# Batch 0 of an attention and token-mixing kernel: w_tok loaded ahead of heads 4 to 7, token mixing on scaled input, both channel-1 halves ahead of channel 2, scores in pairs

## The chip, the cores and the metric

The kernel runs on one core of one Trainium2 chip. The metric is device time in microseconds (us); a kernel's time is the median of its runs. The engines are called as in the profile: PE (TensorE, matrix multiplications), DVE (VectorE), ACT (ScalarE), POOL (GpSimd) and SP (SyncE, which here only issues transfers). Each works through a line of instructions of its own; in the traces below an instruction that waits holds up those behind it on its line (DVE once for 6.83 us). PSUM tiles are the buffers that matmuls write to. The profile is one execution recorded by the hardware profiler.

A run is called fast, or slow when it lies over 1.5% above the fastest run of the same kernel. A ratio below is the mean time of one kernel's fast runs over that of the kernel before's fast runs of the same session, so it is not quite the ratio of the medians that stand beside it. An interval in brackets is a 95% interval.

## The reference, cut to what matters

Four batches, 8 heads, 768 positions, head size 64, model width 512, hidden width 2048.

```python
# block-sorted attention
for _ in range(5):                        # on the 8x8 matrices P (Sinkhorn)
    P = exp(P - max(P)); P /= P.sum(-1) ; P /= P.sum(-2)
k_sorted = einsum('bhij,bhjcd->bhicd', P, k_blocks)       # the same for v
x = softmax(q_block @ k_sorted_block.T / 8) @ v_sorted_block
# mixing, on x of shape (4, 768, 512)
a1  = alpha1 * x + beta1
tok = einsum('ts,bsd->btd', w_tok, a1)                    # token mixing
u   = x + lam * tok
ch  = relu((alpha2 * u + beta2) @ w_ch1) @ w_ch2          # channel 1 (h), channel 2 (ch)
out = u + lam * ch
```

## The kernel before

The program is written out in PE's order. Batch 0 runs as fast as its inputs arrive; from then on the channel mixing of one batch is interleaved with the attention of the next. Cuts are marked.

The loads of batch 0, all issued by POOL, one behind the other: q, then v and k (each in two halves of four heads), then w_tok.

```python
load_q(0)
load_raw(0, 1)              # v, heads 0-3, heads 4-7
load_raw(0, 0)              # k, heads 0-3, heads 4-7
# ...
pool.dma_start(wt16[0:96, :, :], moe_w_tok[0:TAIL, :]. ...)
pool.dma_start(wt16[96:128, :, :], moe_w_tok[TAIL:S, :]. ...)
```

The head of the program. `sc0(h4, g, n)` and `pv0(h4, g, n)` are scores and value sums of a pair of heads; `n` is a number of filler matmuls (identity times identity, thrown away) ahead of them.

```python
mix_k0(0); mix_k0(1)
sc0(0, 0, 1); turn_v0(1, dve.tensor_copy); sc0(0, 1, 1)
mix_k0(2)
pv0(0, 0); sc0(1, 0, 1); turn_v0(2, dve.tensor_copy); pv0(0, 1); sc0(1, 1, 1)
mix_k0(3)
# ... sort_wtok (DVE copies wtp<-wt) and prep_wtok (transposes of w_tok) ...
prep_affine()               # two POOL operations, a1l and b1l
# ...
pv0(3, 0, 2)
# ...
pv0(3, 1, 2)
prep_rs()                   # row sums of w_tok, 36 matmuls with a column of ones
```

Token mixing multiplies plain x; scaling and the row term come afterwards. POOL prepares `u = b1l * rs + x` ahead of time, DVE does the rest.

```python
def moe_tok(b, kts, done=False):
    # ... tok_part(b, kt): 6 matmuls 128x512 into tok_ps, then
    dve.tensor_tensor(tps, tps, a1lB[:], ALU.mult)
    dve.tensor_tensor(u32[kt][:], tok_of[(b, kt)], u32[kt][:], ALU.add)
    act.copy(u16_of[b][:, kt, :], u32[kt][:])
```

The softmax here doesn't subtract the row's maximum and nothing guards it: scores larger than these inputs give would overflow.

## Time and profile before

| | before |
|---|---|
| time, median (range) | 269.02 us (268.73 to 269.40) |
| span of the profiled run | 266.8 us |
| PE busy | 257.3 us, 96% |
| first real work of PE (projection pj) | 11.34 us |
| first token-mixing matmul (tok0) | 33.80 us |
| first channel-1 matmul (h) | 42.47 us |
| last matmul ends | 262.49 us |

The page of the profile first gives each engine's busy time, then the span in 40 slices of 6.7 us: a digit is the busy share in tenths, and PEclk is the clock granted to PE in tenths of full speed. From the page of the kernel before:

```profile
PE 257.3 (96%) x2049; PEld 141.6 (53%) x2059; DVE 154.8 (58%) x333; ACT 125.8 (47%) x232; POOL 92.6 (35%) x100
PE   7799999999999999999999999999999999999993
PEclk9999999999999999999999999999999999999999
```

PE is full in all slices but the first two and the last, and its clock is never lowered. The chain of waits that ended last agrees:

```profile
PE 89%; ACT 4%; DVE 4%; issue 1%; DMA 1%; DVEq 0%; ACTq 0%
```

The next view gives busy time in stretches of the run: from the projection to the first token mixing (tok0), to h, to the token mixing of batch 2 (tok2; tok1 is that of batch 1), to that of batch 3 (tok3), and to the last matmul. Columns: length; busy us of PE, of weight loads, of DVE, ACT and POOL; granted clock; DMA share; GB/s. The kernel before:

```profile
11.34:33.80 22.46, 20.91 (x404) 16.06 (x405) 16.96 (x39) 14.54 (x23) 10.97 (x15) 1.00 1.22 220
33.80:42.47 8.67, 8.67 (x55) 4.20 (x52) 7.14 (x15) 5.79 (x10) 7.78 (x8) 1.00 1.16 210
42.47:143.86 101.39, 100.87 (x809) 55.86 (x813) 64.52 (x129) 53.37 (x100) 44.03 (x45) 1.00 1.07 152
143.86:202.64 58.78, 58.47 (x420) 30.71 (x420) 35.11 (x71) 28.25 (x53) 16.43 (x13) 1.00 0.42 71
202.64:262.49 59.85, 59.69 (x322) 31.04 (x323) 21.98 (x38) 19.95 (x40) 4.16 (x4) 1.00 0.19 49
```

From h on PE is busy for 219.0 of 220.0 us. In the head, the loads set the pace: about 210 GB/s throughout. Two lines of the kernel before's timeline (start, duration), the DVE copies that sort w_tok and the token mixing of batch 1:

```profile
24.53 0.97 DVE L65 COPY wtp<-wt 128x1152 f16<-128x1152 f16 x2
...
85.09 7.93 PE L65 MATMUL tok_ps<-x,w_tokT 128*128 128x512 f16 x36
```

### The profile page before, as it was taken

How to read it: one execution, taken by the hardware profiler on the slowest of the kernel's cores; microseconds unless marked ns; L12 is line 12 of the kernel's file. 1: busy time of each engine (PE TensorE's matmuls, PEld its weight loads, DVE VectorE, ACT ScalarE, POOL GpSimd, SP SyncE). 2: the span in 40 equal slices, each digit the busy share in tenths (PEclk: the TensorE clock that was granted, in tenths of full speed). 3: DMA queues.
4: the chain of work that ended last, by engine and by line, in shares of the span. 5: the costliest groups of instructions: out<-in, count | busy, mean ns of one | idle time of the engine just before them, and what ended most of it. 6: DMA issues, size and time to landing. Idle time of an engine off the chain costs nothing.

```text
span 266.8 us, 5147 instructions
## 1 busy us (share of the span) xinstructions
PE 257.3 (96%) x2049; PEld 141.6 (53%) x2059; DVE 154.8 (58%) x333; ACT 125.8 (47%) x232; POOL 92.6 (35%) x100
## 2 busy tenths in 40 slices
PE   7799999999999999999999999999999999999993
PEld 3467745565565444554565444554565445545542
DVE  6878687639567966722585867704675962042033
ACT  3376767642585312980375404970474305505600
POOL 8524789103585615008918125002409000000000
PEclk9999999999999999999999999999999999999999
DMA  6999999989999544499996342492200422012012
GB/s 80 183 208 252 206 211 207 209 209 118 206 165 146 115 83 120 115 83 95 207 196 135 61 100 80 118 109 51 81 1 2 86 71 79 2 39 79 2 39 79
DMA packets 62423, 30.88 MB, mean 116 GB/s; under 512 B 48888, under 2 KB 58112, under 8 KB 62400
## 3 DMA queue, kind: packets, MB, share of 16 engines
q0 software_dynamic: 23024, 15.60, 39.1%
q1 hardware_dynamic: 39376, 14.96, 32.7%
q8 instruction: 16, 0.26, 0.4%
q14 instruction: 7, 0.06, 0.1%
HBM read 32.78 MB, written 8.65 MB: 155 GB/s over the span
## 4 chain that ended last, share of the span: by engine, by line
PE 89%; ACT 4%; DVE 4%; issue 1%; DMA 1%; DVEq 0%; ACTq 0%
PE ch_ps L65 31%; PE h_ps L65 30%; PE tok_ps L65 12%; PE x_ps L65 5%; PE sc_ps L65 4%; ACT kT L65 2%; PE v_ps L65 2%; PE k_ps L65 1%; PE q_ps L65 1%; ACT et L65 1%; DVE csum L65 1%; DVE P L65 1%; PE m_ps L65 1%; DVE rsum L65 1%; PE wtok_ps L65 1%
## 5 line engine op out<-in xcount | busy, mean ns | idle before, releaser
L65 PE MATMUL h_ps<-a2T,W1p 128*128 128x384 bf16 x512 | 93.4, 326 | 0.2
L65 ACT ACTIVATE hTa<-h_ps 128x384 bf16<-128x384 f32 x96 | 45.9, 492 | 67.7 <-PE h_ps L65 66.6
L65 PE MATMUL ch_ps<-W2p,hTa 128*128 128x512 bf16 (+2 forms) x290 | 65.9, 370 | 0.5
L65 PEld LDWEIGHTS <-W1p 128*128 128x128 bf16 x512 | 47.5, 98 | 30.3 <-issue 0.9
L65 DVE TENSOR_TENSOR ch_ps<-ch_ps,lamB 128x512 f32<-128x512 f32 (+2 forms) x25 | 16.9, 676 | 62.8 <-PE ch_ps L65 60.1
L65 POOL TENSOR_SCALAR u<-b1lB,rs 128x512 f32<-128x512 f32 x18 | 28.9, 1612 | 64.7 <-DVE ost L65 60.1
L65 PEld LDWEIGHTS <-hTa 128*128 128x128 bf16 x300 | 28.7, 98 | 32.4
L65 PE MATMUL tok_ps<-x,w_tokT 128*128 128x512 f16 x144 | 32.1, 379 | 0.0
L65 POOL TENSOR_TENSOR u<-x,u 128x512 f32<-128x512 f16 x22 | 25.4, 1190 | 18.2 <-DVE x L65 17.3
L65 ACT ACTIVATE et<-sc_ps 96x768 f16<-96x768 f32 x32 | 24.9, 807 | 11.7 <-PE sc_ps L65 11.7
L65 ACT CAST u<-u 128x512 f16<-128x512 f32 x24 | 14.8, 618 | 25.7 <-DVE u L65 25.7
L65 PE MATMUL ch_ps<-W2p,hTb 128*128 128x512 bf16 (+2 forms) x100 | 25.0, 371 | 0.0
L65 PEld LDWEIGHTS <-w_tokT 128*128 128x128 f16 x180 | 14.8, 97 | 16.1
L65 DVE TENSOR_TENSOR tok_ps<-tok_ps,a1lB 128x512 f32<-128x512 f32 x24 | 16.6, 693 | 7.7 <-PE tok_ps L65 7.6
L65 DVE CAST kT<-k_ps 64x512 f16<-64x512 f32 x24 | 16.5, 688 | 3.4 <-PE k_ps L65 3.0
L65 DVE TENSOR_TENSOR x<-x_ps,recip 96x512 f16<-96x512 f32 (+2 forms) x32 | 17.6, 554 | 0.9
L65 DVE TENSOR_TENSOR u<-tok_ps,u 128x512 f32<-128x512 f32 x24 | 16.4, 689 | 1.7
L65 ACT ACTIVATE hTb<-h_ps 128x384 bf16<-128x384 f32 x32 | 15.3, 497 | 3.8 <-PE h_ps L65 3.4
L65 DVE TENSOR_TENSOR ost<-ch_ps,u 128x512 f32<-128x512 f32 (+2 forms) x25 | 16.6, 665 | 0.6
L65 POOL DMA_DIRECT2D qn<-in_q_dram x18 | 15.4, 872 | 4.2 <-PE q_ps L65 3.4
L65 PEld LDWEIGHTS <-hTb 128*128 128x128 bf16 x100 | 9.6, 98 | 10.9
L65 PEld LDWEIGHTS <-et 96*128 96x128 f16 (+2 forms) x288 | 12.4, 99 | 4.6 <-issue 1.2
(95 smaller groups left out, 214.0 us busy)
## 6 DMA issues: line engine op xcount, KB each, us to landing
out_dram<-ost SPq DMA_DIRECT2D x23, 192.0 KB, 2.2
raw<-in_v_dram POOLq DMA_DIRECT2D x8, 384.0 KB, 8.2
raw<-in_k_dram POOLq DMA_DIRECT2D x8, 384.0 KB, 10.7
vscr<-vA SPq DMA_DIRECT2D x6, 384.0 KB, 4.4
Vs<-vscr SPq DMA_DIRECT2D x6, 384.0 KB, 7.5
W1p<-in_moe_w_ch_dram POOLq DMA_DIRECT2D x4, 512.0 KB, 10.5
W2p<-in_moe_w_ch_dram POOLq DMA_DIRECT2D x4, 512.0 KB, 18.6
qn<-in_q_dram POOLq DMA_DIRECT2D x12, 128.0 KB, 5.8
```

What stands on the lines that cost most here:

```text
L65: ins = getattr(self.eng, name)(*args, **kwargs)
```

## The change

Its intent is to have real work in place of fillers in the head, and less work on DVE and POOL: w_tok is wanted earlier, so its transposes can fill PE's gaps; token mixing can start on the first columns while the last pair of heads is unfinished; and `a1 = alpha1*x + beta1` is applied to the input (`xa`, times lam and scaled up by 1024, meant to keep the precision of the small factors in f16), which makes row sums, the row term and two POOL operations per tile needless. Scores go in pairs of 16 matmuls, so that PE enters a group of scores half as often. The diff, cut to its core:

```diff
+    LAM_UP = 1024.0
-    load_q(0)
-    load_raw(0, 1)
-    load_raw(0, 0)
+    load_q0(0)                       # then the identity is built, then q's other parts
# ... seven fillers ahead of the projection gone; two groups of q's transposes moved ahead of it
+    load_raw0(0)                     # k and v, heads 0-3
     pool.dma_start(wt16[0:96, :, :], ...)
     pool.dma_start(wt16[96:128, :, :], ...)
+    load_raw0(1)                     # k and v, heads 4-7
# ... fillers of the head gone; scores of batch 0 in pairs; POOL scales heads 0-3:
+        if h4 < 3:
+            aff0(h4 - 1, pool)
+    def affine(b, lo, hi, eng, kts=slice(0, NT)):
+        eng.tensor_tensor(xa, x, a1l16[:, lo:hi] ..., ALU.mult)
+        eng.tensor_tensor(xa, xa, b1l16[:, lo:hi] ..., ALU.add)
# ... batches 1 to 3: scaling on DVE behind the last heads of attention
         def gather(lo, hi):
             for a in range(3):
                 dve.tensor_copy(x128[96:128, a:a + 4:3, lo:hi], ...)
+            affine(b, lo, hi, dve)
# ... token mixing
-                dve.tensor_tensor(tps, tps, a1lB[:], ALU.mult)
-                dve.tensor_tensor(u32[kt][:], tok_of[(b, kt)], u32[kt][:], ALU.add)
+            dve.scalar_tensor_tensor(
+                u32[kt][:], tok_of[(b, kt)], 1.0 / LAM_UP, x_of[b][:, kt, :], op0=ALU.mult, op1=ALU.add
+            )
# ... batch 0: column halves, PSUM tiles shared by kt 0/1 and 2/3
+    for kt in range(NT):
+        tok_part(0, kt, 0, C // 2)
# ... order behind h(0,0)
-    for kk in range(2):
-        moe_ch(0, 0, (kk,))
-        mix_k(1, gs=((0, 1), (2,))[kk])
-        for h4 in range(2 * kk, 2 * kk + 2):
-            turn_q(1, h4, dve.tensor_copy)
+    for n in range(3):
+        moe_h(0, 1, range(2 * n, 2 * n + 2))
+        mix_k(1, gs=(n,), share=(2, 0, 2))
+        turn_q(1, n, dve.tensor_copy)
+    turn_q(1, 3, dve.tensor_copy)
```

## The prediction

> **What bounds it now.** TensorE. The page has PE busy 257.3 of 266.8 us, and the chain of waits is 89% PE. By the timeline, PE starts real work at 11.3 us (the normalised sort matrix is ready), token mixing at 33.8 us, channel-1 (h) at 42.5 us; its last matmul starts after 262.1 us and the last store is issued at 264.2 us. From 42.5 to 262.5 us (220.0 us) PE is nearly gapless: counts times start-to-start times (128x384 0.1625 us, 128x512 0.216, scores 0.039, ...) give about 214 us, so only some 6 us are overhead there. The largest named part is entering a group of scores: 24 entries cost 3.7 us, 0.10 us each where nothing else waits, 0.3 us where a PSUM buffer is late. [...] Before 42.5 us PE is padded with filler matmuls, and the DMA engines are full from about 4 us on, at some 0.2 MB/us.
>
> **Removed from PE before h.** Ten filler matmuls (about 2.3 us), 36 row-sum matmuls (0.9 us), two q transposes' groups moved into the normalisation, small idle gaps: about 3.7 us, if nothing else waits.
>
> **Added before h.** (a) The identity is built after one DMA issue (0.78 us), and DVE copies `pick` before the first reduction: normalisation ends about 0.5 us later. (b) w_tok (1.18 MB) now goes ahead of heads 4 to 7. Landings before: q 9.7, v 13.7, k 17.6, w_tok 23.5 us. At the same rate heads 4 to 7 land at about 21.4 us (k) and 23.2 us (v), where k and v were complete at 17.6. PE, in order, should idle 2 to 3 us at the mixing of k for pair 2. Behind v there are still about 17 us of PE work to h. (c) With both column halves of token mixing ahead of the transposes, the first h waits about 0.5 us for a2T. Summed with trace durations, h starts at about 42.9 us (41.5 to 44.2), against 42.5: the saving is eaten by the DMA order.
>
> **After h starts.** Paired scores: 12 entries for 24; 3.7 us become about 2.2 us ([...]some waits of the second pair for two exponentials of 0.7 us each): -1.3 us. DVE loses one 0.69 us operation per token tile and gains f16 scaling; POOL loses nearly all (54 us): off the critical path, worth about 0. Both channel-1 halves first: same PE work; W2 needed later. Tail: the last two stores go out on two queues: -0.4 us.
>
> **Sum.** +0.4 -1.3 -0.4 = about -1.3: 267.6 us, range 264.9 to 270.6. Faster by over 2%: 0.08; within: 0.88; slower: 0.04.
>
> **What would show it.** Right: a PE wait of 2 us or more for DMA before m_ps near 19 to 21 us; first h between 41.5 and 44; sc groups of 16 entered 12 times after h starts, at about 0.10 us, with fewer us lost than before; DVE and POOL busy much lower without effect; last store on ACT's queue. Wrong: no DMA wait at m_ps, h starting by 40 us.
>
> **What would make it wrong.** The DMA stream starting or running faster than before (then up to 3 us more gain, near 264); long waits of token mixing for POOL's scaling (two 128x768 operations per pair, estimated 2 us each from 1.2 us for 128x512), or of W1's last parts, whose issue stands behind that POOL work; paired scores waiting longer for PSUM.

Two passages are cut out of it: a sentence that gave a reason for the 0.10 us of an entry into scores, which no run here shows, and, in the bracket behind "about 2.2 us", the term of 12 entries at that 0.10 us, 1.2 us in all. The sum is +0.4 us to h, -1.3 us for paired scores and -0.4 us for the tail, about -1.3 us, so 267.6 us (3.7 less 2.2 us is 1.5; 1.3 went into the sum). The 0.10 us itself is in the trace of the kernel before: counted from the start of the matmul ahead and the usual spacing of its kind, scores start 0.09 us late in the median of the 24 entries behind h, 0.29 us at most. The exponentials of scores there take 0.81 us each, 0.70 us from start to start.

## More of the kernel before

Output goes through two buffers, and its stores go out on SP's queue, the one that also carries the transposes of q and of u.

```python
ost = att.tile([128, C], FT, name="ost", tag="ost", bufs=2)
# ... 16 matmuls into cps (ch_ps)
dve.tensor_tensor(cps[:], cps[:], lamB[:, lo:hi], ALU.mult)
dve.tensor_tensor(ost[:, lo:hi], cps[:], u_of[b][kt][:, lo:hi], ALU.add)
nc.sync.dma_start(out[b, kt * 96:(kt + 1) * 96, lo:hi], ost[0:96, lo:hi])
nc.sync.dma_start(out[b, TAIL + kt * 32:TAIL + (kt + 1) * 32, lo:hi], ost[96:128, lo:hi])
```

## The result, and the profile after

The changed kernel takes 293.22 us (292.17 to 296.61, 4 runs) against 269.20 us beside it; the ratio is 1.088 [1.084, 1.092]. The prediction, 267.6 us with a range to 270.6, was 25.6 us too low. The change also spread the times: the four runs of the kernel before beside it lie within 0.7 us; the changed kernel, run twice, ranges from 287 to 297 us.

Both profiles of the changed kernel fell on runs that are called slow by the rule above (296.6 us, and 293.8 us in the second session).

The page of the changed kernel:

```profile
PE 263.5 (89%) x2038; PEld 150.7 (51%) x2051; DVE 149.4 (51%) x324; ACT 127.2 (43%) x232; POOL 42.5 (14%) x62
PE   6787897899899958969999999989999899999994
PEclk9968559999999977999999999999999999999999
```

The work saved is there: POOL fell from 92.6 to 42.5 us, DVE from 154.8 to 149.4. But PE has holes all along the first half, and in slices 3 to 6 and 15, 16 its clock is lowered. The chain that ended last has lost its simplicity:

```profile
PE 51%; DMA 18%; DVE 16%; ACT 6%; POOL 5%; issue 2%; SPq 1%; DVEq 0%; ACTq 0%; POOLq 0%
```

The same stretches as above, in the changed kernel:

```profile
12.60:41.49 28.89, 23.66 (x347) 19.68 (x347) 20.50 (x40) 15.53 (x23) 14.18 (x16) 0.63 1.03 169
41.49:54.38 12.89, 10.47 (x87) 8.55 (x86) 5.15 (x14) 3.09 (x5) 2.28 (x4) 0.89 1.18 204
54.38:169.82 115.44, 103.56 (x808) 56.73 (x814) 61.83 (x129) 55.87 (x105) 15.09 (x22) 0.97 1.05 114
169.82:230.74 60.92, 57.55 (x415) 30.64 (x419) 34.00 (x69) 28.48 (x52) 0.00 (x0) 1.00 0.52 83
230.74:290.60 59.86, 59.70 (x321) 31.04 (x324) 18.27 (x32) 19.42 (x38) 0.00 (x0) 1.00 0.19 49
```

Three stretches lost: to tok0 6.4 us, from tok0 to h 4.2 us, from h to tok2 14.1 us; the projection starts 1.26 us later, and tok2 to tok3 lost 2.1 us. The last stretch is the same to 0.01 us. The largest of PE's waits (total us, times, longest us), where the kernel before had none over 0.4 us after the projection:

```profile
PE tok_ps L66 <- DVE xa L66: 3.8, 3, 1.9
PE tok_ps L66 <- DVE ost L66: 3.4, 1, 3.4
PE k_ps L66 <- DVE vA L66: 3.3, 2, 2.1
PE wtok_ps L66 <- DVE wtp L66: 3.3, 3, 1.7
...
PE tok_ps L66 <- DVE u L66: 1.6, 2, 0.8
...
PE m_ps L66 <- DMA raw<-in_k_dram: 0.9, 1, 0.9
```

With the smaller ones, PE's waits from the projection on add up to some 22 us. The stretches above say the same: from the projection to the last matmul PE is idle for 23.1 us, against 2.5 us before. On top of that its busy time grew by 6.3 us, although fillers and row sums are gone; that part is half speed. In the changed kernel's stretches from 12 to 44 us, read finely, the clock is at exactly half for two long times:

```profile
14.00:20.00 6.00, 5.97 (x88) 5.05 (x89) 3.29 (x8) 3.86 (x6) 0.00 (x0) 0.50 1.18 207
...
26.00:28.00 2.00, 0.28 (x3) 0.28 (x4) 1.97 (x4) 0.50 (x1) 2.00 (x2) 0.79 1.02 169
28.00:44.00 16.00, 14.48 (x153) 11.79 (x151) 12.21 (x27) 6.90 (x9) 10.21 (x13) 0.50 0.86 144
```

So "busy" deceives here: PE is busy for 23.7 us of the first stretch against 20.9 before, with fewer matmuls (347 against 404), because many of them run at half speed: twelve matmuls of m_ps take 0.85 us at 16.43 us, at a clock of 0.50, and 0.53 us at 22.02 us, at 1.00. In this profile the clock is at 0.50 from 13.5 to 20.3 us and from 27.2 to 44.2 us. How much of a run is at half varies (the clock of the first stretch is 0.63 in this profile and 0.76 in the second), and so does the wait of PE that goes before it. The clock falls behind waits of 3.1 us (no_fill) and 3.9 us (wtok_early), below. But here no single wait between 14 and 44 us is over 1.73 us, and the clock is at 0.50 for 16 us from 28 us on, with PE busy for 14.5 of the 16; 5 us of PE without a gap from 28.3 us on did not end it. What sets the clock is not shown by these runs.

The first of these two times is in every profile of the changed head, whatever was mended in it. In all sixteen of them (windows of 0.25 us) the clock falls to half between 11.6 and 15.7 us, for 3.41 or 6.83 us, ahead of PE's waits for k and for the sorted w_tok; in the four profiles with the old head (before, pair_before, no_fill, wtok_early) it stays at 1.00 until 20 us. It costs an estimated 1.7 or 3.4 us, half its length, as the clock is at half. The change took two things away around that place, the seven fillers right ahead of the projection and the two groups of q's transposes behind it, and no run puts them back: why the clock falls there was not tested.

Two places of the changed kernel's timeline show what PE waited for. First, DVE sorting w_tok while POOL scales x:

```profile
24.11 1.63 POOL L66 TENSOR_TENSOR xa<-x,a1l 128x768 f16<-128x768 f16 x1 [10.36 <-DVE x L66]
24.85 2.81 DVE L66 COPY wtp<-wt 128x1152 f16<-128x1152 f16 x2
25.82 1.72 POOL L66 TENSOR_TENSOR xa<-xa,b1l 128x768 f16<-128x768 f16 x1
```

Two copies that took 0.97 us before take 2.81 us and end when POOL's pair of operations ends. Second, the token mixing of batch 1, where SP's queue holds six transposes of q for 28.8 us, with six output stores behind them:

```profile
79.63 28.81 SPq L143 DMA_TRANSPOSE qT<-qn  x6
...
104.47 4.15 PE L66 MATMUL tok_ps<-xa,w_tokT 128*128 128x512 f16 x12 [1.86 <-DVE xa L66]
108.54 4.21 SPq L700 DMA_DIRECT2D out_dram<-ost  x6
111.24 0.69 DVE L66 TENSOR_TENSOR ost<-ch_ps,u 128x512 f32<-128x512 f32 x1 [6.83 <-DMA out_dram<-ost]
111.99 7.03 PE L66 MATMUL tok_ps<-xa,w_tokT 128*128 128x512 f16 x24 [3.37 <-DVE ost L66]
```

PE waits first for the scaling (1.86 us), then for DVE, which stands 6.83 us at an output buffer whose store has not left. Before, the 36 matmuls took 7.93 us in one go.

### The profile page after: what moved, and what is told of

It reads as the page before. It is cut to its first block, busy times and chain, and to the rows that moved or that the text cites. A ratio compares the mean times of both kernels' runs of the same rounds, so it can differ in the third digit from the quotient of the medians.

```text
span 294.8 us, 5035 instructions
## 1 busy us (share of the span) xinstructions
PE 263.5 (89%) x2038; PEld 150.7 (51%) x2051; DVE 149.4 (51%) x324; ACT 127.2 (43%) x232; POOL 42.5 (14%) x62
## 4 chain that ended last, share of the span: by engine, by line
PE 51%; DMA 18%; DVE 16%; ACT 6%; POOL 5%; issue 2%; SPq 1%; DVEq 0%; ACTq 0%; POOLq 0%
PE ch_ps L66 17%; PE h_ps L66 16%; PE tok_ps L66 10%; DMA qn<-in_q_dram 8%; DMA a2T<-u 4%; DMA raw<-in_k_dram 4%; DVE x L66 3%; DVE xa L66 2%; PE x_ps L66 2%; ACT et L66 2%; DVE wtp L66 2%; POOL qn L66 2%; DVE kT L66 2%; PE k_ps L66 2%; ACT kT L66 2%
## 5 line engine op out<-in xcount | busy, mean ns | idle before, releaser
L66 PE MATMUL ch_ps<-W2p,hT 128*128 128x512 bf16 (+2 forms) x387 | 84.6, 370 | 0.5
L66 ACT ACTIVATE hT<-h_ps 128x384 bf16<-128x384 f32 x128 | 60.6, 496 | 37.9 <-PE h_ps L66 37.1
L66 PEld LDWEIGHTS <-hT 128*128 128x128 bf16 x400 | 38.0, 98 | 41.8
L66 PE MATMUL tok_ps<-xa,w_tokT 128*128 128x512 f16 (+1 forms) x180 | 36.7, 367 | 8.8 <-DVE xa L66 3.8
L66 ACT CAST u<-u 128x512 f16<-128x512 f32 x24 | 14.7, 618 | 50.9 <-DVE u L66 50.9
L66 DVE SCALAR_TENSOR_TENSOR u<-tok_ps,x 128x512 f32<-128x512 f32 x24 | 16.3, 688 | 13.3 <-PE tok_ps L66 13.3
L66 PE MATMUL x_ps<-Vs,et 96*128 96x65 f16 (+2 forms) x288 | 16.3, 205 | 1.1 <-ACT et L66 0.7
L66 DVE TENSOR_SCALAR a2T<-a2T,ab2col 128x384 bf16<-128x384 f16 x24 | 7.5, 376 | 13.4 <-DMA a2T<-u 13.4
L66 PEld LDWEIGHTS <-raw 128*64 128x64 f16 (+1 forms) x168 | 8.9, 123 | 8.5 <-issue 6.2
L66 ACT CAST kT<-k_ps 64x512 f16<-64x512 f32 x16 | 9.3, 580 | 4.8 <-PE k_ps L66 4.6
L66 PEld LDWEIGHTS <-kT 64*96 64x96 f16 x256 | 7.7, 132 | 6.1 <-ACT et L66 1.9
```

The costliest lines, as they stand in the source:

```text
L66: ins = getattr(self.eng, name)(*args, **kwargs)
```

## The experiments

Eighteen kernels were run. Theory: the head lost its clock because the fillers went, and behind h the loss comes from DVE and SP lines which used to be off the critical path. Rivals: the order of loads, the added scaling, the pairing of scores, the reordered channel parts. One table for all; each row's profile gives the starts, in us. "clock" is PE's granted clock from the projection to tok0.

| kernel | median us | ratio to before | clock | h starts | h to tok2 | tok2 to tok3 |
|---|---|---|---|---|---|---|
| before | 269.0 | 1 | 1.00 | 42.47 | 101.39 | 58.78 |
| changed, 1st | 293.2 | 1.088 | 0.63 | 54.38 | 115.44 | 60.92 |
| changed, again (a_again) | 291.4 | 1.070 | 0.76 | 52.29 | 116.04 | 59.57 |
| aff_dve | 291.5 | 1.083 | 0.79 | 49.12 | 116.80 | 59.57 |
| tok_tiles | 290.3 | 1.069 | 0.74 | 48.52 | 115.42 | 59.57 |
| raw_first | 291.5 | 1.080 | 0.73 | 51.59 | 114.30 | 59.57 |
| warm | 287.0 | 1.065 | 0.88 | 52.84 | 107.78 | 59.57 |
| head_fix | 288.8 | 1.074 | 0.93 | 47.58 | 114.96 | 59.58 |
| stores_first | 293.3 | 1.089 | 0.69 | 51.99 | 115.02 | 59.57 |
| stores_pool | 289.7 | 1.075 | 0.75 | 51.70 | 114.20 | 59.57 |
| q2_whole | 289.1 | 1.071 | 0.87 | 49.87 | 111.04 | 63.99 |
| ost4 | 288.3 | 1.068 | 0.80 | 50.11 | 111.44 | 59.57 |
| order_back | 288.3 | 1.072 | 0.81 | 51.04 | 109.27 | 60.44 |
| best1 | 280.7 | 1.045 | 0.93 | 46.21 | 106.28 | 62.96 |
| post_scale | 277.4 | 1.018 | 0.87 | 47.29 | 103.12 | 64.22 |
| post_again | 279.2 | one run | unknown | 0.87 | 46.96 | 103.12 | 63.18 |
| post_ost | 277.9 | 1.019 | 0.87 | 47.36 | 103.06 | 58.78 |
| pair_before | 269.6 | 1.002 | 1.00 | 42.66 | 102.26 | 59.69 |
| no_fill | 269.6 | 1.000 | 0.93 | 44.39 | 101.39 | 58.78 |
| wtok_early | 280.4 | 1.042 | 0.84 | 51.68 | 101.38 | 58.78 |

A warning on how to read it: a_again, stores_first, stores_pool and ost4 have the same head program, and their h starts at 50.1 to 52.3 us, at clocks of 0.69 to 0.80. One profile of a head like this is worth no more than 2 us. In time, no single edit stands clear of the changed kernel: its two sessions gave 1.088 and 1.070, and the ten edits of it from aff_dve to order_back 1.065 to 1.089. Only best1 and the kernels built on it do.

### The changed kernel again (a_again)

> The changed kernel again, for a profile in the fast state. Expected 292 to 294 us; first h near 54 us, token mixing of batch 1 starting near 104 us with a wait on the store buffer ost, granted clock well under 1 before 50 us and near 105 to 115 us.

No edit. It gave 291.37 us (287.26 to 294.75): the spread is the kernel's own. The waits are those of the first profile, and the granted clock differs (0.76 for 0.63), so the same program draws different amounts of half speed.

### Output stores ahead of the transposes of q (stores_first)

```diff
-        with tc.issue_after(regroup[b - 1].ins):
+        with tc.issue_after((stored[0, 2] if b == 2 else regroup[b - 1]).ins):
# ... and in moe_ch, stored[b, kt] keeps each store
```

> Only edit: on the DMA queue of SP the six transposes of q(2) are put behind the six output stores of batch 0's first half; every compute engine's order is unchanged. Theory (stores stand in line behind transposes that wait for q(2), DVE waits for the store buffer, PE for DVE): the 6.8 us wait of ost on the stores and the 3.4 us wait of tok on it vanish, token mixing 1 to token mixing 2 falls from 65 us to 57 or less, time falls by 6 to 9 us. Rival (late data for q(2) or DVE's order alone is to blame): time within 2 us of the changed kernel.

It gave 293.27 us. DVE's wait for output buffers vanished, but now the transposes of q stood among those of u, DVE waited 7.9 us for u's transposes, and the stretch was as long as before. The wait only moved along SP's line.

### Scaling on DVE and not on POOL (aff_dve)

```diff
-            aff0(h4 - 1, pool)
+            aff0(h4 - 1, dve)
```

> Only edit: the scaling of heads 0 to 3 goes from POOL to DVE. Theory (POOL's two long operations slow the DVE copies that sort w_tok): the three pairs of copies wtp<-wt fall from 2.8, 2.3, 1.3 us to about 1.0, 0.7, 0.9 us, PE's waits on wtp from 3.3 us to under 1, first h from 54.4 to about 50 us, time by 3 to 5 us. Rival (the copies are late because w_tok lands late): the pairs keep their length and the time stays within 1.5 us.

The copies that sort w_tok took 0.62, 0.62 and 0.83 us a pair in place of 2.81, 2.29 and 1.29 us. One of those lines of its timeline:

```profile
25.82 0.62 DVE L66 COPY wtp<-wt 128x1152 f16<-128x1152 f16 x2
```

So POOL's scaling did hold DVE up. The copies of 2.81 us ended within 0.12 us of the end of POOL's second operation; by what means the one engine holds up the other is not shown. The time is 291.48 us all the same: h starts at 49.1 us, but the later stretches are as long as ever.

### Fillers put back into the changed head (warm)

```diff
         pair = [psa([128, 2, 4, 128], FT, "sc_ps") for _ in range(2)]
+        spin(pair[0][:, 0, :, :].rearrange("p i x -> p (i x)"), 3)
...
-        pv_tiles(h4, g, ets[(h4, g)])
+        pv_tiles(h4, g, ets[(h4, g)], 2)
```

> Only edit: 28 filler matmuls of 512 columns (6 us of PE time at full clock) before the score pairs and the x tiles of batch 0. Theory (PE's gaps lose it the clock, and the lost clock costs more than the gaps): granted clock over 0.95 from 14 to 50 us, a 256-column tok matmul near 0.107 us instead of 0.145, first h 2 to 5 us earlier. Rival (the clock costs little, PE waits for others anyway): first h later by 1 to 6 us.

28 fillers raised the clock from about 0.75 to 0.88, at full speed from 22 us on, and h started at 52.84 us, in the same range as without. To within the 2 us of the warning above, some 6 us of thrown-away work cost nothing and gained nothing, so neither the theory (h 2 to 5 us earlier, clock over 0.95) nor the rival is borne out. All 28 stand behind the place where the clock first falls (13.4 us here), so that half clock stayed. The time, 287.04 us, is better than a_again's, but by the stretch behind h (107.8 us), where the program is the same. That stretch became the next question.

### Batch 2's q loaded earlier (q2_whole)

```diff
# ... ahead of the last matmuls of h(0, 0)
-    pool.tensor_copy(gate[:], Vs[1][0:1, 0, 0:2])
-    load_raw(2, 1)
-    load_raw(2, 0)
# ... behind turn_q(1, 3)
+    load_q(2)
+    pool.tensor_copy(gate[:], Vs[1][0:1, 0, 0:2])
+    load_raw(2, 1)
+    load_raw(2, 0)
...
-            load_q(2)
```

> Only edit: the load of q(2) goes out whole, ahead of the loads of k and v of batch 2 (in the changed kernel its last two of six parts stand behind those four); nothing else is reordered. Theory (in stores_first the line on SP only moved: q(2)'s transposes, late for their data, then stood in front of the transposes of u that DVE waits for; what is late is q(2)'s last two parts): the transposes of q(2) end by 92 us instead of 99 to 108, before the first store is due; no wait on ost or on u's transposes over 4 us; token mixing 1 to 2 falls from 65.9 us to 56 to 58 us, time by 7 to 9 us against the changed kernel. Rival (DVE's order and the added evictions make this stage long): it stays over 62 us.

289.10 us. The transposes of q still ran from 75.3 to 99.5 us. Part of the loss moved from the stretch before tok2 to the one after it (64.0 us). From tok1 to tok2 it took 60.96 us, between what the theory and what the rival expected. A miss.

### PSUM tiles of token mixing not shared (tok_tiles)

```diff
-            if b == 0 and kt in (0, 2):
-                pair = psa([128, 2, C], FT, "tok_ps")
-                # ... kt and kt + 1 are halves of one tile
+            tok_of[(b, kt)] = (psa if b == 0 and kt < 2 else psb)([128, C], FT, "tok_ps")[:]
```

> Only edit: the six token-mixing results of batch 0 get a PSUM tile each instead of two pairs sharing a tile (and the first transposes take the other pool). Theory (PE waits twice 0.78 us for DVE's read of the other half of the same tile, which it doesn't touch): both waits go, tok to first h falls from 11.57 us to about 9.5, about 2 us. Rival (DVE is the limit there): unchanged within 0.5 us.

The two waits of 0.78 us for `u` are gone, and tok0 to h fell from 11.58 to 9.81 us: with a shared tile, the second column half of one kt had to wait until DVE had read the other. What is left above the 8.67 us of before is a wait of 0.99 us for a2T. 290.31 us in all.

### Heads 4 to 7 ahead of w_tok in the changed kernel (raw_first)

```diff
+    load_raw0(1)
     pool.dma_start(wt16[0:96, :, :], ...)
     pool.dma_start(wt16[96:128, :, :], ...)
-    load_raw0(1)
```

> Only edit: k and v of heads 4 to 7 are loaded ahead of w_tok again. Theory of the prediction (this order costs 2 to 3 us of PE wait): the waits of m_ps for DMA (2.1 and 0.3 us) go, but the sorting copies may now wait for w_tok (landing near 23.5 us); token mixing starts 1 to 3 us earlier. Rival (the head is limited by the lost clock and by DVE behind POOL): first h moves by less than 1 us.

The wait for k at m_ps (2.1 us in a_again) went, PE waited 3.9 us for the sorted w_tok (3.2 in a_again), and tok0 started at 38.4 us instead of 40.7. The clock stayed at 0.73 and fell again behind tok0, so h started at 51.6 us: no clear gain, 291.47 us. Within a head that has other waits, the order of loads cannot be judged; wtok_early below judges it in a head that has none.

### Paired scores alone, in the kernel before (pair_before)

```diff
-        prev = [emit_scores(b, 0, g) for g in range(2)]
+        prev = emit_pair(b, 0)
         for h4 in range(1, H4):
-            cur = [emit_scores(b, h4, g) for g in range(2)]
+            cur = emit_pair(b, h4)
# ... emit_pair and its added dependencies, as in the changed kernel
```

> The kernel before with one part of the change alone: scores of batches 1 to 3 issued in pairs of 16. Theory: [...]waits of the second pair give back up to 0.8; time 0.3 to 1.5 us below before. Rival (pairs wait longer for PSUM than they save): 0 to 1.5 us above.

The gain: 12 entries fewer at 0.10 us each, 1.2 us.

269.63 us, ratio 1.002 [0.999, 1.005]. Half the entries into scores are saved, and in each of the two stretches behind tok1 PE waits some 1.5 us that it had not waited: 1.0 us for DVE's x in the first, 0.9 us for DVE's bigV in the second, and the rest for copies and exponentials of ACT. Paired scores are neither the loss nor a gain.

### Batch 0's stores on another queue (stores_pool)

```diff
-                    to.dma_start(out[b, at:at + r1 - r0, lo:hi], ost[r0:r1, lo:hi])
+                    (nc.gpsimd if b == 0 else to).dma_start(out[b, at:at + r1 - r0, lo:hi], ost[r0:r1, lo:hi])
```

> Only edit: the twelve output stores of batch 0 are issued from POOL's queue, which is idle then, instead of from SP's; no compute engine's order changes. Theory (what costs is standing in one line on SP: q(2)'s transposes are slow whatever their data's order, 24 us in q2_whole too[...]): with the stores in another line DVE no longer waits for ost, tok no longer for DVE's ost; token mixing 1 to 2 falls from 65.9 us to 56 to 58.5 us, 7 to 9 us. Rival (DVE's own work in this order, with the DMA engines busy, makes the stage long): stays over 62 us.

289.66 us. With the stores elsewhere, the six transposes of q still took 28.2 us on SP's queue, so stores don't slow them; and the stretch h to tok2 is 114.2 us: DVE still waited twice for an output buffer, once for 2.8 us and at 152 us for 3.2 us, now one of batch 1, whose stores had stayed on SP, and PE's waits for `xa` (1.9 us) and `vA` (2.0 us) stayed too.

### The old order of channel parts (order_back)

```diff
-    for n in range(3):
-        moe_h(0, 1, range(2 * n, 2 * n + 2))
-        mix_k(1, gs=(n,), share=(2, 0, 2))
-        turn_q(1, n, dve.tensor_copy)
+    for kk in range(2):
+        moe_ch(0, 0, (kk,))
+        mix_k(1, gs=((0, 1), (2,))[kk])
+        # ... as in the kernel before
```

> One part undone: batch 0's channel 2 of the first half goes back ahead of channel 1 of the second half, as before; head, scaling and pairs stay changed. Theory (this reordering is what puts six stores and eight DVE evictions behind the transposes and in front of token mixing 1): from first h to token mixing 2 the changed kernel takes 116.0 us and the kernel before 101.4; this one should take 102 to 105 us, time 10 to 13 us below the changed kernel. Rival (the scaled input on DVE is what delays token mixing 1 and 2): over 109 us.

h to tok2 fell from 114 to 116 us to 109.3 us: the transposes of q ran as one of 1.3 us and five of 7.4 us, late (89 to 97 us), as in the kernel before. What was left is a wait of 4.66 us for the scaled input `xa` at tok1, and a clock of 0.94 from the first scores to tok1. The 102 to 105 us of the theory were missed, and the rival's mark (over 109 us, the scaled input on DVE) was just met. 288.31 us.

### Four mends of the head at once (head_fix)

The edits of aff_dve and tok_tiles, the identity built before the first load and `pick` copied later, and 16 fillers (two ahead of each pair of scores, one ahead of each value sum).

```diff
+        spin(pair[0][:, 0, :, :].rearrange("p i x -> p (i x)"), 2)
...
+        if it == 1:
+            dve.tensor_copy(pick, ident16[0:CT, 0:CT].unsqueeze(2).to_broadcast([CT, CT, 128]))
```

> Changed kernel with the head mended only: scaling on DVE, a PSUM tile for each token-mixing result, the identity built before the first load again with pick copied later, and 16 fillers (3.5 us at full clock) against the loss of the clock. Theory: pj at 11.4 us, clock over 0.95 to the first h, first h at 43 to 46 us instead of 50 to 54. The rest as in the changed kernel (236 to 238 us from first h to the end); time near 280.

The projection starts at 11.89 us (12.60), h at 47.58 us at a clock of 0.93; 288.79 us. The head regained about 4 us of its 8 to 10 in the profile; the time did not follow (ratio 1.074, a_again's 1.070). h at 43 to 46 us, a clock over 0.95 and a time near 280 us were all missed.

### All mends found so far (best1)

head_fix, raw_first, order_back, and scores unpaired.

```diff
-        prev = emit_pair(b, 0)
+        prev = [emit_one(b, 0, g) for g in range(2)]
...
     load_raw0(0)
+    load_raw0(1)
     # ... w_tok
-    load_raw0(1)
```

> All mends at once: head as in head_fix with k and v of heads 4 to 7 ahead of w_tok again, channel order as before, scores single. If the parts found are all there is, first h at 40 to 44 us and 220 to 222 us from there: 264 to 270 us, level with before. If something else is hidden: over 273.

280.74 us (279.74 to 283.29), ratio 1.045 [1.041, 1.049]. This is the first version that is clearly faster than the changed kernel, and still 11.6 us are missing. PE now waits 2.9 us for `xa` at tok1, and the 36 token-mixing matmuls behind it take 9.28 in place of 7.93 us.

### The kernel before without its fillers (no_fill)

```diff
-        spin(sps[:, 0, :, :].rearrange("p i x -> p (i x)"), spins)
...
-        spin(bank, spins)
```

> The kernel before with nothing taken out but its ten filler matmuls in the head (six ahead of scores of batch 0, four ahead of its value sums). They occupy about 3 us of TensorE (0.31 us each, start to start). Theory (the fillers keep the granted clock up, and it is their loss that lets the clock fall to half in the changed head): the clock between the projection and the first token mixing falls below 0.95, that stage grows from 22.5 us to 23 us or more, and the time to 270.5 us or more or at least its spread grows. Rival (the clock falls in the changed head because of its real waits for data, and fillers that stand where nothing waits are a mere cost): clock stays at 1.00, the stage shrinks to 20 to 22 us and the time to 267 to 269 us.

269.59 us, ratio 1.000 [0.997, 1.003]. Two stretches of its profile:

```profile
24.00:27.00 3.00, 0.05 (x3) 0.00 (x0) 0.86 (x3) 0.88 (x2) 1.83 (x3) 1.00 1.16 218
...
28.00:32.00 4.00, 4.00 (x56) 3.62 (x53) 3.36 (x10) 2.13 (x3) 2.96 (x4) 0.57 1.23 203
```

PE runs ahead, stands for 3.1 us until w_tok has landed and been sorted, and behind that wait its clock is at 0.57 for 4 us. tok0 is 1.9 us later in this profile, and the median 0.4 us. So both the theory and its rival were partly wrong: without these fillers the clock does fall, but the stretch they fill is spare time that a load (w_tok) sets, and losing them alone cost 1.9 us in this profile and nothing clear in the median. Dropping these ten is not the main loss of the change. The seven fillers ahead of the projection, which the change dropped too, stood in place here, so their loss is not tested. In this run the kernel before waits for w_tok, which makes the idea of loading it earlier look sound.

### One load moved, in the kernel before (wtok_early)

```diff
-            for hh in range(2):
+            for hh in range(1 if kv == 0 else 2):
# ... behind the two loads of w_tok:
+    load_raw_half(0, 1)              # k, heads 4-7
```

> The kernel before with one load moved: the second half of k of batch 0 (heads 4 to 7, 384 KB) is issued behind w_tok (1152 KB) and not ahead of it. In the profile before, these loads land one after the other at 15.7 (k, first half), 17.7 (k, second half) and 23.6 us (w_tok), and the third head pair's k is wanted at 19.3 us. Theory (the head lives on the bandwidth of its loads, so an order that puts w_tok first only moves the wait to the heads): TensorE waits 3 to 4.5 us for k at the third m_ps, the clock may fall to half after it, the first token mixing starts at 36 to 38 us in place of 33.8 and the time is 271 to 273.5 us. Rival (the early w_tok pays back what k loses, since its sorting and transposes can then fill that wait): they stand later in TensorE's fixed order, so this could only be true if nothing is lost at all; time 268.5 to 270.5 us.

280.38 us (277.79 to 280.53), ratio 1.042 [1.038, 1.045]: far above both expectations. The move of one load of 384 KB costs 11 us in the median. The profile is of the fastest of the six runs and shows 9.2 us of it, all in the head: behind h every stretch is the kernel before's to 0.01 us. Its stretches, and then the place in its timeline where the chain goes on:

```profile
20.00:23.40 3.40, 0.02 (x2) 0.02 (x2) 0.00 (x0) 0.37 (x1) 1.53 (x2) 0.90 1.19 303
23.40:30.00 6.60, 6.60 (x82) 4.79 (x83) 2.85 (x7) 2.39 (x4) 4.72 (x7) 0.53 1.20 203
...
35.00:40.00 5.00, 3.60 (x33) 2.76 (x33) 3.51 (x10) 2.90 (x4) 0.23 (x1) 0.66 1.09 205
```

```profile
23.38 0.85 PE L65 MATMUL m_ps<-bigH,raw 128*64 128x128 f16 x12 [3.86 <-DMA raw<-in_k_dram]
...
31.07 0.63 DVE L65 COPY wtp<-wt 128x1152 f16<-128x1152 f16 x2
32.31 3.41 DVE L65 COPY wtp<-wt 128x1152 f16<-128x1152 f16 x2
32.73 1.28 POOL L65 TENSOR_TENSOR a1lB<-a1lB,lamB 128x512 f32<-128x512 f32 x1
33.96 1.26 POOL L65 TENSOR_TENSOR b1lB<-b1lB,lamB 128x512 f32<-128x512 f32 x1
...
36.24 0.90 PE L65 MATMUL vt_ps<-ident,vT 128*96 128x128 f16 x8 [1.66 <-DVE w_tokT L65]
```

This shows in one run what a wait in the head can set off. PE waits 3.9 us for k, as expected. Then the clock is at 0.53 for 6.6 us, which costs an estimated 3 us (0.47 of 6.6). The delay pushes DVE's sorting of w_tok into POOL's `prep_affine`, which it used to miss: two copies take 3.41 us where the two ahead of them took 0.63, PE waits 1.7 us for the copy that stands behind them on DVE's line, and the clock falls once more (0.66 from 35 to 40 us). A wait of 4 us became a delay of 9.2 us at tok0 and h. The changed head has more waits than this one, so how much of its loss goes this way is not shown: raw_first took its wait for k away, and h came no earlier.

### Four output buffers in place of two (ost4)

```diff
-            ost = att.tile([128, C], FT, name="ost", tag="ost", bufs=2)
+            ost = att.tile([128, C], FT, name="ost", tag="ost", bufs=4)
```

> The changed kernel with four output buffers (ost) in place of two and nothing else. In its profiles VectorE waits 5.9 to 6.8 us in two places for a store to leave an output buffer, and TensorE then waits for VectorE. Theory (the stores behind the transposes of q on SyncE's queue hold the output buffers, VectorE stands in line for them, and the 7 us that the stage from the second to the third token mixing loses come from there): VectorE's wait for output buffers goes away, the stage falls from 64 to 66 us to 58 to 60 us, and the time to 284 to 287 us. Rival (as moving the stores showed, the wait only moves to another instruction in VectorE's line): stage 63 us or more, time 289 to 293 us.

288.27 us (286.49 to 291.81). DVE's wait for output buffers is gone although the transposes of q take 27.9 us and the stores leave as late as ever (from 103.3 us on), and token mixing of batch 1 runs in one go behind its wait for `xa`:

```profile
75.34 27.89 SPq L143 DMA_TRANSPOSE qT<-qn  x6
...
100.19 7.93 PE L66 MATMUL tok_ps<-xa,w_tokT 128*128 128x512 f16 x36 [1.86 <-DVE xa L66]
```

h to tok2 is 111.4 us, 4.6 us less than in a_again. That DVE's wait comes from late stores is shown; that all of the 4.6 us do is not, since warm, the same program there but for its two buffers, took 107.8 us. In time nothing is gained that is clear (ratio 1.068, a_again's 1.070). The remaining 10 us above the kernel before were not taken apart; the profile has the scaling (1.86 us at tok1), DVE's waits for u's transposes (10.9 us in all) and a clock of 0.97 from tok1 to tok2.

### The old scaling for batches 1 to 3, in best1 (post_scale, post_again, post_ost)

```diff
-            affine(b, lo, hi, dve)                 # in gather, batches 1 to 3
...
+            for kt in range(NT):                   # in moe_start, batches 1 to 3
+                pool.tensor_scalar(u32[kt][:], b1l16[:], rs[:, kt:kt + 1], None, op0=ALU.mult)
+                pool.tensor_tensor(u32[kt][:], x_of[b][:, kt, :], u32[kt][:], ALU.add)
...
+            if b > 0:
+                dve.tensor_tensor(tok_of[(b, kt)], tok_of[(b, kt)], a1l16[:], ALU.mult)
...
+    prep_rs()                                      # behind h(0, 0)
```

> The best mended version so far (280.7 us) with batches 1 to 3 scaled as in the kernel before: token mixing on the plain values, the product multiplied on VectorE afterwards, row term and values added ahead of time on POOL; batch 0 keeps its scaled input. Theory (scaling the input of batches 1 to 3 stands in VectorE's line between attention and token mixing, where TensorE has nothing else to do): the waits for the scaled values (2.9 and 1.2 us) go away, the half clock after them too, the stage up to the second token mixing shortens by 2 to 4 us and the third batch's by 2 to 3 us; time 274 to 277 us, about 1 us of it being given back for 36 added row-sum matmuls. Rival (the waits are caused by something ahead of the scaling, in attention itself): the waits turn up at the plain values instead, time 279 to 283 us.

From the first scores of batch 1 to tok2 PE waits for nothing: h to tok2 is 103.1 us, of which about 1 us are the 36 row sums; best1 had 106.3, the changed kernel 115 to 116. Its time is 277.35 us, from runs in two groups of two, 274 and 280 us. The ratio of 1.018 [1.015, 1.022] counts the fast group alone, and at 2% it is called unclear. The profile fell on one of 280 us, and there the stretch tok2 to tok3 is 64.2 us.

> The same kernel as post_scale, one more look, because two of its four runs took 280 us and two 274 us, and its profile fell on one of 280 us: there TensorE waits 2.5 us ahead of its ninth token-mixing matmul of batch 2 for nothing the profile shows, while three transposes of q took 19.6 us on SyncE's queue, and the clock is at half after it. Theory (that 6 us belongs to a bad draw of the transfers, not to the program): a profile of 272 to 274 us shows stages of 58.8 to 59.9 us for batches 1 to 3 as before, and the remaining difference lies ahead of the second token mixing. Rival: the loss is in every run, only in varying places.

The second look took 279.19 us and lost 4.4 us in the same stretch: five transposes of q took 21.0 us on SP's queue, the last of the six followed, and DVE waited 5.7 us for the transposes of u behind them:

```profile
134.83 21.01 SPq L143 DMA_TRANSPOSE qT<-qn  x5
...
165.02 1.25 DVE L66 TENSOR_SCALAR a2T<-a2T,ab2col 128x384 bf16<-128x384 f16 x4 [5.67 <-DMA a2T<-u]
```

DVE waits for no output buffer in either profile of this kernel, although the next expectation takes that for the cause. So the loss was not a stray one.

> The mended version with the old scaling for batches 1 to 3 (post_scale) and four output buffers in place of two. Both profiles of post_scale lose 4.4 to 5.4 us in the stage from the second to the third token mixing, against 58.8 us before, and have there five or three transposes of q for batch 3 that hold SyncE's queue for some 20 us with output stores behind them. Theory (the loss is output buffers that wait behind those transposes): with four buffers that stage is 58.8 to 60 us in every profile, the runs fall into one group, time 272 to 274.5 us; what remains against 269 us is the head, 3 to 4 us, plus about 1 us of added row sums. Rival (the transposes also delay what token mixing itself needs): the stage keeps 62 us or more, the two groups stay, time 276 to 278 us.

With four output buffers the profile fell on a fast run, and this version's stretches behind h are those of the kernel before, but for 1.7 us (the last one, 59.85 us, is not shown):

```profile
47.36:150.42 103.06, 102.15 (x850) 56.69 (x850) 63.63 (x130) 53.71 (x101) 43.49 (x43) 1.00 0.99 133
150.42:209.20 58.78, 58.58 (x421) 30.73 (x419) 35.13 (x71) 28.25 (x53) 16.42 (x13) 1.00 0.46 79
```

But its six runs still fall into two groups, 274 to 275 us (three) and 281 to 282 us (three); its ratio, 1.019 [1.013, 1.025], is of the three fast ones and again unclear. Output buffers are therefore not the cause of the two groups, and what is stays open. The one profile of the good group has its five transposes of q for batch 3 in 14.7 us, and DVE's wait for u's transposes behind them is 1.4 us; the two of post_scale's bad group had 22.4 and 21.0 us for five, and waits of 3.1 and 5.7 us. That the groups differ by this line is likely, and not tested: no profile of post_ost fell on its bad group.

No version found beats the kernel before. The best runs, 274 us, keep of the change chiefly batch 0's scaled input, its column halves and the loading of small vectors as rows, and the profile of post_ost loses 4.9 us up to h.

### Why the transposes of q are slow

This was read from the traces and not changed by an experiment of its own. The transfers of the stretch from 60 to 110 us, with the median time from issue to landing as last number, in the kernel before:

```profile
raw<-in_v_dram POOLq DMA_DIRECT2D x2, 384.0 KB, 7.6
raw<-in_k_dram POOLq DMA_DIRECT2D x2, 384.0 KB, 10.7
```

and in a_again:

```profile
raw<-in_v_dram POOLq DMA_DIRECT2D x2, 384.0 KB, 16.4
raw<-in_k_dram POOLq DMA_DIRECT2D x2, 384.0 KB, 19.2
```

Before, POOL issues these loads of batch 2 at 66.8 us, and five of the six transposes run at 82.7 us, in 7.5 us. In a_again POOL stands 27 us until PE has turned q of batch 1; then it issues four of the six parts of q(2) and, at 77.6 us, the loads, just as the first transpose starts. Counted from the start of h, the loads go out nearly when they did (25.3 us behind it, 24.3 before). What moved is q(2): its six transposes start 25.2 us behind h, where five of them started 40.2 us behind it. And both drag: a single transpose takes up to 10.0 us, at a median of 1.6. In warm, with the same program, the loads landed in 8.5 and 11.3 us and the six transposes took 19.5 us, the stores left before the buffers ran out, and the stretch was 8 us shorter. In bytes over the time from the first's start to the last's end, waits for their input included, the six transposes of 128 KB ran at about 40 GB/s in warm and at 27 GB/s in the changed kernel (28.8 us), and five of them at 87 GB/s in the kernel before (7.5 us). So the new order puts two groups of transfers on top of each other, and how badly they collide differs from run to run. That they slow each other is a reading of these coincidences, not a test.

## Why the prediction was wrong, point by point

1. **"About 3.7 us, if nothing else waits"** (removed from PE before h). The work did go. Of its largest part, the ten fillers, no_fill shows that it was worth nothing: the time stays at 269.6 us, because PE then stands for w_tok. The rest was not tested alone.
2. **"PE, in order, should idle 2 to 3 us at the mixing of k for pair 2."** The wait is there, at 0.9 us in the first profile, 2.1 in a_again and 3.9 in wtok_early. The failed step is the cost put on it. The sum counted a wait as its own length; wtok_early shows a wait of 3.9 us that moves h by 9.2 us, through half clock and through the collision of DVE with POOL. The sum has no term for the clock at all: the page of before showed 1.00 throughout, which held for that kernel and not for the changed one (0.63 to 0.93 from the projection to tok0). Part of that is not even due to this wait: the clock is at half for 3.41 or 6.83 us before it, in every profile of the changed head.
3. **"h starts at about 42.9 us (41.5 to 44.2)".** It starts at 52 to 54 us in the changed kernel's two profiles, at 50 to 52 in three others with the same head program. Of the failed terms: the projection 1.26 us later, where 0.5 was said; tok0 to h 2.9 us longer (fast profile of stores_pool), where 0.5 was said, of which 1.6 us are waits in shared PSUM tiles that were not seen, and 1.0 us is the wait for a2T; the rest, 5.1 us, is in the stretch to tok0, which has the half clock, the waits of point 2 and POOL's scaling in it; how they share it stays open.
4. **"Long waits of token mixing for POOL's scaling"** was named as a danger. The operation was estimated well, 2 us against 1.63 to 1.72 measured, but the harm was another: POOL's operations stopped DVE's copies (2.81 us for 0.97; 0.62 in aff_dve).
5. **"Off the critical path, worth about 0"** (DVE, POOL behind h) and **"Both channel-1 halves first: same PE work".** This is the largest failed step: 13 us behind h. Work moved from POOL, with time to spare, to DVE's line between attention and token mixing, where PE has to wait for it (`xa`, 3.8 us in all, up to 4.66 us at tok1 in order_back). post_scale undoes this alone in best1: the waits are gone, and the ratio of fast runs falls from 1.045 to 1.018. The order of channel parts was indeed the same PE work, but with it q(2)'s transposes fell on the loads of k and v and held SP's queue for 27 to 29 us with six stores behind them, and DVE stood up to 6.83 us at an output buffer. In the profiles of order_back and ost4, which each take one part of that away, h to tok2 is 109.3 and 111.4 us; their times gain nothing clear. Together the parts are shown: with all of them undone, post_ost's fast profile is within 1.7 us of the kernel before from h to the last matmul. What each was worth is not.
6. **"-1.3 us"** for paired scores. The 12 entries were there as said, and so were waits that the prediction had put at less, for DVE and ACT: pair_before is at 1.002 [0.999, 1.005].
7. **Tail, "-0.4 us".** From the end of the last matmul to the end of the span there are 4.3 us before and 4.2 after. Worth nothing measurable.

A rough account of the 22.8 us between the profiles of before and of stores_pool, a fast run whose only edit is the queue of 12 stores: projection 1.2, to tok0 5.1, to h 2.9, to tok2 12.8, to tok3 0.8, last stretch 0.

What stays open: what sets the clock, and why it first falls at 12 to 16 us in the changed head; the cause of the two groups of times of post_scale and post_ost; how the 12.8 us behind h divide exactly, as the edits overlap and runs of one program differ by 8 us in that stretch; and whether the transposes and the loads would run undisturbed if only their starts were kept apart.

## What to carry to other kernels

Here PE was gapless and at full clock, and the lines of the other engines met the moments at which their results were wanted. In a kernel like that, price a change by what each wait does next (here a clock of 0.53 for 6.6 us behind a wait of 3.9 us, 3.41 us for two copies in place of 0.63 beside another engine's operations, and 6.83 us at an output buffer whose store stood behind transposes) and not by its own length. Before work is moved from an idle engine to a busy one, look at where it lands in that engine's order: ahead of what does PE wait? And test the named idea alone first: one load moved in the old kernel told more than ten mends of the new one, whose times could not be told apart.
